# Computing the first token tile of six experts during the attention phase of a fused attention and mixture-of-experts kernel

## The chip, the core and the metric

The kernel runs on one core of a Trainium2 chip. The metric is the device time of one execution in microseconds (us), the median over the timed runs. The core has a matrix engine (TensorE, PE in the profile), a vector engine (VectorE, DVE), a scalar engine (ScalarE, ACT), a general engine (GpSimd, POOL) and a queue engine (SyncE, SP) that here only issues transfers. Each engine executes its own instructions in the order in which they were laid down; instructions of different engines wait for each other through semaphores.

## What is computed

The reference has two blocks. The first is a gated linear attention: for each of 4 batches and 8 heads a complex 48 by 48 state decays by a per-channel factor and takes in an outer product at each of 768 steps.

```python
mag = np.sqrt(a_re * a_re + a_im * a_im)
scale = np.minimum(mag, 0.999) / (mag + 1e-06)
a_re_n, a_im_n = (a_re * scale, a_im * scale)
for t in range(S):
    ar, ai = (a_re_n[:, :, t, :, None], a_im_n[:, :, t, :, None])
    new_re = ar * S_re - ai * S_im
    new_im = ar * S_im + ai * S_re
    kv = np.einsum('bhd,bhe->bhde', k[:, :, t], v[:, :, t])
    S_re, S_im = (new_re + kv, new_im)
    y[:, :, t] = np.einsum('bhd,bhde->bhe', q[:, :, t], S_re)
```

The output, 3072 tokens of 384 numbers, goes into a mixture of 8 experts. Each token goes to the one expert with the largest of 8 logits; the expert is a two-layer network with a hidden width of 1024.

```python
logits = x @ w_gate
expert_idx = np.argmax(logits, axis=1)
# for each expert e, over the tokens that chose it:
h = np.maximum(x_sorted[lo:hi] @ w1[e], 0.0)
y_sorted[lo:hi] = h @ w2[e]
# in the tokens' own order, times the softmax weight of the chosen expert:
return (gate_w[:, None] * y).astype(np.float32)
```

All of it is in 32-bit floats. A matmul on 32-bit operands stands in the trace as two matmul instructions, so that the 24 matmuls of an expert's first layer are 48 lines of the trace.

## The kernel before

**Attention.** The tokens are cut into 24 tiles of 128 (`NT`); tile `g` is chunk `s = g // 4` of batch `b = g % 4`. Two tiles are a unit (`U = 2`), so there are 12 units, and four tiles, one chunk of all batches, are a group (`GR = 4`). The loop `for u in range(NU + 1)` (L498) is a hand-written software pipeline. In iteration `u` it does the decay work of unit `u + 1` (`decay_steps`, `decay_angle`), the cumulative sums of unit `u` by matmul (`decay_sums`, `angle_sums`: tiles `csl` and `cst`), the sines (`rotation`), and then, for the two tiles of unit `u - 1`, `scores(g)` and, one tile later, `outputs(g - 1)`. `scores` multiplies Q and K by their decays on POOL and DVE (`product`, L317), transposes them on PE through the PSUM pool `psT` (two buffers, one bank each), copies them out on ACT or DVE, and makes the attention block `at`, which DVE masks (L424). `outputs` makes `y` from `am` and the state `G`, transposes it, and computes the router's logits (`logits`, L327). All eight PSUM banks are taken by the attention's pools.

**Routing.** After a group of four tiles, `route` (L355) works out for each token its expert (`choose`), its rank within the expert (a running count `cx` and a matmul with a triangle of ones) and from that the row in a DRAM buffer `xs` with `CAP = 448` rows for each expert. Tokens are written there by `put` (L390), an indirect transfer on POOL, one for each tile; one is issued in each call of `scores` (L408). The last group's `route` is called with `end=True` after the loop (L539): it first sets the counts to at least `FIRST = 256`, so that no token of the last group falls into an expert's first 256 rows. That is what makes the first two tiles of an expert complete ahead of the last group. A row that no token took was blanked beforehand (`blank`) and its result is dropped by the bounds check of the scatter. A token with rank 448 or more would set `ov`, and then a slow path (`others`, L770) would run behind the kernel.

**Experts.** After the attention its pools are closed (L542), and the experts are done one after another (L663). `gather` (L475) reads the expert's rows from `xs`; `turn` (L555) transposes them; `expert` (L579) makes the first layer, `hps`, in 8 slices of the hidden width with 3 accumulating matmuls each, all token columns at once (448 columns; relu on DVE and ACT in turn), and the second layer, `yps`, tile by tile: three full tiles of 128 tokens with 8 matmuls of 384 columns each, and a half tile of 64 tokens whose 8 matmuls run in pairs beside each other. `scatter` (L569) writes each tile of results to its tokens' rows. Expert 0 is done in two parts: tiles 0 and 1 first (256 columns, gathered at L538 before the last group is routed), then the remaining tile and a half (192 columns, `rest0`, L661). Beside experts 1 to 6 run checks of the decay inputs on ACT and POOL (`range_check`, L630).

**Weights.** An expert's weights are 1536 KB for each layer. `load_w` (L153) puts them into one of two buffers, by `e % 2`. Expert 0's are loaded in seven pieces during units 4 to 10 of the attention (L533), expert 1's at the end of the attention, and those of expert `e + 2` when expert `e` is done.

**Order.** The order on each engine is made when the kernel is built: a scheduler takes the instructions by their place in the program and by when they are expected to be ready, so an instruction that is ready may be laid down ahead of one that stands before it in the program. `queue` (L147) forces one instruction behind another. Once built, the order is fixed.

Of the kernel before, what the change touches and what calls it, by code (L numbers as in the profile page):

```python
# [20 lines left out]
P = 128  # L21
# [16 lines left out]
def kernel(  # L38
# [26 lines left out]
    CAP = CT * P - HT  # L65
    FIRST = 2 * P
    NS = E * CAP
    GR = B
# [14 lines left out]
    wp = [ctx.enter_context(tc.tile_pool(name="wp", bufs=1)), None]  # L83
    gp = ctx.enter_context(tc.tile_pool(name="gp", bufs=2))

# [38 lines left out]
    nc.vector.memset(cx[:, 0], 0.0)  # L124
    base = const([P, E], "base")
    rev = const([P, E], "rev")
    nc.gpsimd.iota(rev, pattern=[[-1, E]], base=E, channel_multiplier=0, allow_small_or_imprecise_dtypes=True)
# [24 lines left out]

    def load_w(e, parts=None):  # L153

        if e not in W_T:
            W_T[e] = [
                wp[e % 2].tile([P, n, w], FP, tag=nm, name=nm + "t") for nm, n, w in (("w1", KD, F), ("w2", KF, DM))
            ]
        a, b = W_T[e]
        w1e, w2e = w1[e].rearrange("(i p) f -> p i f", p=P), w2[e].rearrange("(i p) d -> p i d", p=P)  # L160
        if parts is None:
            nc.sync.dma_start(out=a, in_=w1e)
            T["w"] = nc.sync.dma_start(out=b, in_=w2e)
        else:
            for i in parts:
                o, x, i = (a, w1e, slice(i, i + 1)) if i < KD else (b, w2e, slice(2 * (i - KD), 2 * (i - KD) + 2))
                queue(nc.sync.dma_start(out=o[:, i], in_=x[:, i]), T["ld"])
# [6 lines left out]
    un = att.enter_context(tc.tile_pool(name="un", bufs=2))  # L174
    ch = att.enter_context(tc.tile_pool(name="ch", bufs=2))
    psM = att.enter_context(tc.tile_pool(name="psM", bufs=1, space=PSUM))
    psT = att.enter_context(tc.tile_pool(name="psT", bufs=2, space=PSUM))
# [177 lines left out]
    def route(j, end):  # L355
# [3 lines left out]
        tt, ts, stt = nc.vector.tensor_tensor, nc.vector.tensor_scalar, nc.vector.scalar_tensor_tensor  # L359
        choose(j, n)  # L360
        oh = xl.tile([P, n, E], BF, tag="oh", name="oh")
        tt(out=oh, in0=bc(rev, 1, n), in1=bc(fst[:, sl], 2, E), op=OP.is_equal)
# [39 lines left out]
    def scores(g):  # L402
# [4 lines left out]
        K = product(u, c, "K", "k", "Ei")  # L407
        if T["put"]:  # L408
            queue(T["put"].pop(0)(), T["K"])
        qts, ats = [], []  # L410
# [23 lines left out]
    def outputs(g):  # L434
# [38 lines left out]
        logits(xt, g)  # L473

    def gather(s, sizes):  # L475

        n = len(sizes)
        xg = gp.tile([P, n, XW], FP, tag="xg", padded_shape=[P, CT, XW], name="xg")
        f = sum(m == P for m in sizes)
        nc.sync.dma_start(out=xg[:, :f], in_=xs[s : s + f * P].rearrange("(i p) c -> p i c", p=P))  # L480
        if f < n:
            nc.sync.dma_start(out=xg[0 : sizes[f], f], in_=xs[s + f * P : s + f * P + sizes[f]])
        return xg
# [14 lines left out]
    for u in range(NU + 1):  # L498
# [19 lines left out]
        else:  # L518
            table("natural_log_exp_and_others")
            for g in T.pop("done", []):  # L520
                T["put"] += route(g, False)
        for g in range((u - 1) * U, u * U):
            if g >= 0:
                scores(g)
            if g > 0:
                outputs(g - 1)
                if g % B == 0:
                    T["done"] = [g - B]
        if u == 1:
            blank()  # L530
        if u + 2 < NU:
            load_a(u + 2)
        if NU - 8 <= u < NU - 1:  # L533
            load_w(0, [u - (NU - 8)])
    outputs(NT - 1)
    for f in T["put"]:
        f()
    own0 = gather(0, [P] * (FIRST // P))  # L538
    for f in route(NT - GR, True):  # L539
        f()  # L540

    att.close()  # L542


    wp[1] = ctx.enter_context(tc.tile_pool(name="wp1", bufs=1))
    load_w(1)
    xp = ctx.enter_context(tc.tile_pool(name="xp", bufs=2))
# [7 lines left out]
    def turn(sizes, xg):  # L555
# [11 lines left out]
        return xt  # L567

    def scatter(y, idx, m):  # L569
        return nc.gpsimd.indirect_dma_start(  # L570
            out=out,
            out_offset=bass.IndirectOffsetOnAxis(ap=idx, axis=0),
            in_=y[0:m],
            in_offset=None,
            bounds_check=N - 1,
            oob_is_err=False,
        )

# [82 lines left out]
    rest0 = [P] * ((CAP - FIRST) // P) + [HT]  # L661
    own = [P] * (CT - 1) + [HT]
    for e in range(E):  # L663
        if e == 0:
            part = [([P] * (FIRST // P), own0), (rest0, gather(FIRST, rest0))]
        else:
            part = [(own, xg)]
        for i, (sizes, g) in enumerate(part):
            xt = turn(sizes, g)
            if i == len(part) - 1 and e + 1 < E:  # L670
                xg = gather((e + 1) * CAP, own)
            todo = []
            if i == len(part) - 1 and 1 <= e < E - 1:
                todo = [lambda b, i=i: range_check(i, b) for i in range(NC) if i % (E - 2) == e - 1]
            expert(sizes, xt, *W_T[e], g, todo)
        if e + 2 < E:
            load_w(e + 2)
        for i in range(NC):
            if i % (E - 2) == e:
                range_load(i)  # L680
        if e == E - 2:
            verdict()
# [152 lines left out]
```

## Time and profile before

| | |
|---|---|
| median of three runs | 647.17 us |
| span of the profiled execution | 648.5 us |
| PE busy | 577.9 us (89%) |
| ACT, DVE, POOL busy | 277.8, 238.3, 215.0 us |
| DMA | 79.74 MB, mean 123 GB/s |
| last logits of the attention copied out (DVE L336) | at 327.0 us |
| first expert's first `hps` matmul | at 327.5 us |
| last matmul | ends at about 638.5 us |

A busy time on PE runs from the start of a matmul to the end of its results, and consecutive matmuls overlap; the distance from one start to the next is shorter than the duration that a row gives. The page also lists the share of the full TensorE clock that was granted (PEclk).

A unit of the attention is followed in the trace by its second sine on ACT (`CS<-f`), which appears once in each unit. For units 6 to 11 these start at 173.8, 195.4, 225.3, 246.9, 279.1 and 298.8 us (times rounded). Right after its second sine a unit's `scores` begin, which stand in iteration `u + 1` of the loop, where the change puts `first` and `second` ahead of them. A stretch from one such time to the next holds one unit's worth of work; the last stretch runs from 298.8 us to the first expert. These six stretches are where the six early tiles would lie.

### The profile page before, as it was taken

How to read it: one execution, taken by the hardware profiler on the slowest of the kernel's cores; microseconds unless marked ns; L12 is line 12 of the kernel's file. 1: busy time of each engine (PE TensorE's matmuls, PEld its weight loads, DVE VectorE, ACT ScalarE, POOL GpSimd, SP SyncE). 2: the span in 40 equal slices, each digit the busy share in tenths (PEclk: the TensorE clock that was granted, in tenths of full speed). 3: DMA queues.
4: the chain of work that ended last, by engine and by line, in shares of the span. 5: the costliest groups of instructions: out<-in, count | busy, mean ns of one | idle time of the engine just before them, and what ended most of it. 6: DMA issues, size and time to landing. Idle time of an engine off the chain costs nothing. (4 is left out here: it accounts for less than half of the span.)

```text
span 648.5 us, 8554 instructions
## 1 busy us (share of the span) xinstructions
PE 577.9 (89%) x3319; PEld 378.7 (58%) x3319; DVE 238.3 (37%) x487; ACT 277.8 (43%) x467; POOL 215.0 (33%) x206
## 2 busy tenths in 40 slices
PE   1496989889699699799999999999999999999993
PEld 0184767668478477588776555555555555555551
DVE  2354657547557547658231211212121021211210
ACT  4656964763666466475210115152341614225100
POOL 3544155351563553632212105032140512405111
PEclk9998899969899899899989999999999999999998
DMA  9999864652743813205203543735425373430000
GB/s 163 210 340 178 124 131 80 151 108 50 159 109 75 161 39 75 62 14 196 73 26 107 201 150 118 252 109 210 137 80 207 109 261 110 152 114 25 10 12 30
DMA packets 151673, 79.74 MB, mean 123 GB/s; under 512 B 130134, under 2 KB 141927, under 8 KB 151624
## 3 DMA queue, kind: packets, MB, share of 16 engines
q1 hardware_dynamic: 143168, 63.75, 41.3%
q0 software_dynamic: 4736, 15.20, 6.9%
q10 hardware_dynamic: 3720, 0.16, 0.4%
q8 instruction: 28, 0.46, 0.3%
q14 instruction: 21, 0.17, 0.1%
HBM read 63.74 MB, written 15.98 MB: 123 GB/s over the span
## 5 line engine op out<-in xcount | busy, mean ns | idle before, releaser
L75 PE MATMUL hps<-xt,w1t 128*128 128x448 f32 (+2 forms) x432 | 148.1, 503 | 0.0
L75 PE MATMUL yps<-w2t,ht 128*128 128x384 f32 (+1 forms) x512 | 147.2, 488 | 0.3 <-DVE y L603 0.3
L75 PEld LDWEIGHTS yps<-w2t,ht 128*128 128x128 f32 (+1 forms) x512 | 81.4, 177 | 64.5 <-issue 15.0
L75 PEld LDWEIGHTS hps<-xt,w1t 128*128 128x128 f32 x432 | 80.8, 192 | 61.8 <-issue 58.7
L588 ACT ACTIVATE ht<-hps 128x448 f32<-128x448 f32 (+2 forms) x36 | 18.1, 502 | 136.1 <-PE hps L75 136.1
L75 PE MATMUL at<-qt,kt 96*128 96x128 f32 x384 | 57.1, 295 | 18.1 <-ACT qt L78 9.4
L75 PEld LDWEIGHTS at<-qt,kt 96*128 96x128 f32 x384 | 50.3, 203 | 28.8 <-ACT qt L78 12.9
L570 POOL DMA_INDIRECT out_dram<-y,xg x32 | 30.9, 967 | 93.0 <-DVE y L603 44.6
L641 POOL TENSOR_TENSOR cs<-cs,cw 128x768 f32<-128x768 f32 x12 | 21.6, 1804 | 117.4 <-ACT cw L637 117.4
L592 DVE TENSOR_SCALAR ht<-hps 128x448 f32<-128x448 f32 (+2 forms) x36 | 20.6, 573 | 103.4 <-PE hps L75 103.4
L603 DVE TENSOR_SCALAR y<-yps,xg 128x384 f32<-128x384 f32 x24 | 14.8, 617 | 118.4 <-PE yps L75 118.4
L320 POOL TENSOR_TENSOR Qe<-q,E 128x384 f32<-128x384 f32 x24 | 23.9, 997 | 82.3 <-ACT E L185 68.6
L75 PE MATMUL y<-am,v 128*64 128x128 f32 x384 | 49.1, 288 | 0.0
L424 DVE TENSOR_TENSOR am<-at,tri 128x512 f32<-128x512 f32 x48 | 33.0, 688 | 33.3 <-PE at L75 33.1
L75 PE MATMUL csl<-A,tri_half 128*128 128x384 f32 x48 | 24.8, 602 | 21.1 <-DVE A L238 18.5
L391 POOL DMA_INDIRECT xs<-x,to x24 | 24.4, 1016 | 57.2 <-DMA xs<-x,to 39.3
L75 PE MATMUL y<-qt,G 96*64 96x128 f32 x320 | 42.1, 280 | 0.0
L416 PE MATMUL tp<-ident,Q 128*96 128x128 f32 x192 | 34.2, 298 | 3.7 <-DVE Q L324 3.7
L75 PE MATMUL dk<-v,K 128*96 128x48 f32 x320 | 33.9, 259 | 2.4 <-DVE t L454 2.4
L75 PEld LDWEIGHTS y<-am,v 128*64 128x64 f32 x384 | 30.0, 138 | 9.7 <-issue 7.4
L78 ACT COPY qt<-tp 96x512 f32<-96x512 f32 x48 | 27.0, 581 | 20.1 <-PE tp L416 18.8
L191 ACT ACT_TABLE_LOAD x27 | 34.6, 1283 | 2.2 <-PEq L821 0.8
(123 smaller groups left out, 805.9 us busy)
## 6 DMA issues: line engine op xcount, KB each, us to landing
w1t<-in_moe_w_dram SPq DMA_DIRECT2D x7, 1536.0 KB
w2t<-in_moe_w_dram SPq DMA_DIRECT2D x7, 1536.0 KB
xs<-zrow POOLq DMA_DIRECT2D x1, 5404.0 KB, 22.4
ar<-in_a_re_dram SPq DMA_DIRECT2D x12, 384.0 KB
ai<-in_a_im_dram SPq DMA_DIRECT2D x12, 384.0 KB
q<-in_q_dram SPq DMA_DIRECT2D x12, 384.0 KB
k<-in_k_dram SPq DMA_DIRECT2D x12, 384.0 KB
v<-in_v_dram SPq DMA_DIRECT2D x12, 384.0 KB
```

What stands on the lines that cost most here:

```text
L75: return nc.tensor.matmul(o, lhsT=lhsT, rhs=rhs, start=start, stop=stop, skip_group_check=True)
L78: (nc.scalar.copy if i % 2 else nc.vector.tensor_copy)(out=o, in_=in_)
L191: ins = nc.scalar.preload_act_table_set(name)
L320: T[nm] = nc.gpsimd.tensor_tensor(out=e.rearrange("p h d -> p (h d)"), in0=T[src, u][:, sl], in1=T[dec, u][:, sl], op=OP.mult)
L391: return nc.gpsimd.indirect_dma_start(out=xs[:, :], out_offset=bass.IndirectOffsetOnAxis(ap=to[:, i : i + 1], axis=0), in_=x[:, i], in_off ...
L416: nc.tensor.transpose(out=tp[0:DD, j], in_=X[:, hg * 4 + j], identity=ident)
L424: nc.vector.tensor_tensor(out=am, in0=at, in1=bc(tri, 1, 4), op=OP.mult)
L570: return nc.gpsimd.indirect_dma_start(out=out, out_offset=bass.IndirectOffsetOnAxis(ap=idx, axis=0), in_=y[0:m], in_offset=None, bounds_ch ...
L588: relu = nc.scalar.activation(out=ht[:, f], in_=ps, func=AF.Relu)
L592: nc.vector.tensor_scalar(out=ht[:, f], in0=ps, scalar1=0.0, scalar2=None, op0=OP.max)
L603: nc.vector.tensor_scalar(out=y, in0=ps, scalar1=gate, scalar2=None, op0=OP.mult)
L641: nc.gpsimd.tensor_tensor(out=s, in0=s, in1=w, op=OP.add)
```

## The change

It computes the first tile of 128 tokens of the experts 0 to 5 (`EARLY`) within the attention phase, one expert in each of the loop's iterations 7 to 12, and takes these tiles out of the expert phase. For this the first tile has to be complete early. After two groups (1024 of the 3072 tokens) are routed, the third `route` sets the counts of the six experts to at least 128 (the tile is closed), so that later tokens go to later rows. The purpose is to use time that PE spends waiting in the attention phase.

The parts are these. The tile is read from `xs` by `early_gather`, issued in the iteration before. `first` does its three transposes, one copy on ACT, 24 matmuls of 128 columns for the first layer (the result in two tiles of `psT`, each emptied by one relu, on ACT and on DVE), and it stands ahead of the first `scores` of the iteration. `second` does 8 matmuls of 384 columns, one DVE multiplication by the gate and a scatter, and stands ahead of the second `scores`. The weights of experts 0 to 5 go one after another through a single buffer during the attention. Since expert 5's are there when the attention ends, the expert phase begins with expert 5, goes on with 6 and 7, and then does 0 to 4, whose weights are loaded a second time. In the expert phase the six experts have 320 columns in place of 448 and two full tiles in place of three. Expert 5's first part is now a single tile of 128, its second part is as expert 0's was. Puts are issued two for each `scores` in the first four groups, and the pool `gp` of the gathered tiles is opened after the attention's pools are closed.

```diff
+    EARLY = range(6)
...
-    def load_w(e, parts=None):
-
-        if e not in W_T:
+    def load_w(e, parts=None, buf=0, new=True):
+
+        if new:
             W_T[e] = [
-                wp[e % 2].tile([P, n, w], FP, tag=nm, name=nm + "t") for nm, n, w in (("w1", KD, F), ("w2", KF, DM))
+                wp[buf].tile([P, n, w], FP, tag=nm, name=nm + "t") for nm, n, w in (("w1", KD, F), ("w2", KF, DM))
             ]
...
+        if j == 2 * GR:
+
+            pc = psL.tile([P, E], FP, tag="mm", padded_shape=[P, 512], name="pc")
+            mm(pc, ones_b, cx[:, j])
+            ts(out=base, in0=pc, scalar1=float(P), scalar2=-float(P), op0=OP.min, op1=OP.add)
+            ne = len(EARLY)
+            stt(out=cx[:, j, :ne], in0=base[:, :ne], scalar=lead, in1=cx[:, j, :ne], op0=OP.mult, op1=OP.add)
...
-        if T["put"]:
-            queue(T["put"].pop(0)(), T["K"])
+        for _ in range(2 if g < 4 * B else 1):
+            if T["put"]:
+                queue(T["put"].pop(0)(), T["K"])
...
+    def early_gather(e):
+        xg = fl.tile([P, XW], FP, tag="xg", name="fxg", bufs=2)
+        queue(nc.sync.dma_start(out=xg, in_=xs[e * CAP : e * CAP + P]), T["ld"])
+        T["fx", e] = xg
+
+    def early(e):
...
+        def first():
+            tp = psT.tile([P, 4, P], FP, tag="tp", name="ftp")
+            for d in range(KD):
+                nc.tensor.transpose(out=tp[:, d], in_=xg[:, d * P : (d + 1) * P], identity=ident)
+            xt = fl.tile([P, KD, P], FP, tag="xt", name="fxt")
+            nc.scalar.copy(out=xt, in_=tp[:, 0:KD])
+            for z in range(2):
+                ps = psT.tile([P, 4, P], FP, tag="tp", name="fhp")
+                for i in range(4):
+                    f = 4 * z + i
+                    for d in range(KD):
+                        mm(ps[:, i], wa[:, d, f * P : (f + 1) * P], xt[:, d], d == 0, d == KD - 1)
+                if z:
+                    nc.vector.tensor_scalar(out=ht[:, 4:8], in0=ps, scalar1=0.0, scalar2=None, op0=OP.max)
+                else:
+                    nc.scalar.activation(out=ht[:, 0:4], in_=ps, func=AF.Relu)
+
+        def second():
+            ps = psT.tile([P, 4, P], FP, tag="tp", name="fyp").rearrange("p a b -> p (a b)")[:, :DM]
+            y = fl.tile([P, DM], FP, tag="y", name="fy", bufs=2)
+            for f in range(KF):
+                mm(ps, ht[:, f], wb[:, f], f == 0, f == KF - 1)
+            nc.vector.tensor_scalar(out=y, in0=ps, scalar1=xg[:, DM : DM + 1], scalar2=None, op0=OP.mult)
+            scatter(y, xg[:, DM + 1 : DM + 2].bitcast(I32), P)
...
+        e = u - 7
+        if e >= 0:
+            steps = early(e)
         for g in range((u - 1) * U, u * U):
+            if e >= 0:
+                steps[g % U]()
...
-        if NU - 8 <= u < NU - 1:
-            load_w(0, [u - (NU - 8)])
+        if 3 <= u < 7:
+            load_w(0, [2 * u - 6, 2 * u - 5] if u < 6 else [6], new=u == 3)
+        if 6 <= u < NU:
+            early_gather(u - 6)
+        if 7 <= u < NU:
+            load_w(u - 6)
     outputs(NT - 1)
     for f in T["put"]:
         f()
-    own0 = gather(0, [P] * (FIRST // P))
+    att.close()
+    gp = ctx.enter_context(tc.tile_pool(name="gp", bufs=2))
+    order = [EARLY[-1], *range(len(EARLY), E), *EARLY[:-1]]
+    own0 = gather(order[0] * CAP + P, [P] * (FIRST // P - 1))
     for f in route(NT - GR, True):
         f()
...
-    for e in range(E):
-        if e == 0:
-            part = [([P] * (FIRST // P), own0), (rest0, gather(FIRST, rest0))]
-        else:
-            part = [(own, xg)]
+    xg = own0
+    for n, e in enumerate(order):
+        own = [P] * (CT - 2 if e in EARLY else CT - 1) + [HT]
+        part = [(own, xg)]
+        if n == 0:
+            part = [([P] * (FIRST // P - 1), xg), (rest0, gather(e * CAP + FIRST, rest0))]
...
-        if e + 2 < E:
-            load_w(e + 2)
+        if n + 2 < E:
+            load_w(order[n + 2], buf=n % 2)
```

## The prediction

> **What bounds the kernel now.** I read first the busy times in stretches (one row for each attention unit from the sixth on, then the handover to the experts, then the experts). Columns: stretch, its length, busy us and count of PE, weight loads, DVE, ACT, POOL, granted clock, DMA share, GB/s.
>
> ```profile
> 173.80:195.40 21.60, 19.41 (x183) 14.88 (x179) 12.53 (x21) 15.18 (x27) 11.70 (x11) 1.00 0.45 99
> 195.40:225.30 29.90, 24.97 (x226) 19.85 (x226) 19.30 (x44) 15.52 (x28) 12.65 (x12) 0.94 0.60 116
> 225.30:246.90 21.60, 19.44 (x183) 14.92 (x180) 12.51 (x21) 15.15 (x27) 11.98 (x11) 1.00 0.21 44
> 246.90:279.10 32.20, 28.60 (x250) 23.14 (x250) 20.57 (x47) 17.23 (x32) 13.96 (x13) 0.89 0.34 75
> 279.10:298.80 19.70, 19.70 (x182) 15.60 (x184) 11.97 (x24) 12.43 (x24) 7.35 (x9) 1.00 0.09 20
> 298.80:327.50 28.70, 26.11 (x275) 21.04 (x272) 12.53 (x38) 11.99 (x25) 4.14 (x5) 0.98 0.38 140
> 327.50:349.50 22.00, 22.00 (x85) 15.96 (x84) 5.67 (x28) 1.76 (x5) 5.08 (x6) 0.95 0.17 59
> 349.50:367.20 17.70, 17.29 (x88) 12.52 (x86) 3.28 (x8) 1.64 (x5) 1.95 (x2) 1.00 0.44 145
> 367.20:648.50 281.30, 270.20 (x872) 143.99 (x870) 45.99 (x83) 82.77 (x139) 71.40 (x53) 0.99 0.36 126
> ```
>
> The experts are bound by PE alone. The attention is bound mostly by PE as well: the six units take 153.7 us, of which PE is busy 138.2, and the next engine, DVE, 89.4. One unit (19.7 us) has no PE idle time at all; the long ones (29.9, 32.2) have 3.6 to 4.9 us.
>
> Next, the timeline of PE in an expert (start, us, matmuls):
>
> ```profile
> 407.94 18.31 PE L75 MATMUL hps<-xt,w1t 128*128 128x448 f32 x48
> 426.08 18.37 PE L75 MATMUL yps<-w2t,ht 128*128 128x384 f32 x64
> 444.38 2.22 PE L561 MATMUL tp<-ident,xg 128*128 128x128 f32 x12
> 446.54 18.31 PE L75 MATMUL hps<-xt,w1t 128*128 128x448 f32 x48
> ```
>
> An expert takes 446.54 - 407.94 = 38.6 us without a gap. Last, the handover, on PE and on POOL:
>
> ```profile
> 339.17 10.48 PE L75 MATMUL yps<-w2t,ht 128*128 128x384 f32 x32
> 349.49 0.94 PE L561 MATMUL tp<-ident,xg 128*128 128x128 f32 x4
> 351.30 8.07 PE L75 MATMUL hps<-xt,w1t 128*128 128x192 f32 x48
> ```
>
> ```profile
> 333.75 0.97 POOL L391 DMA_INDIRECT xs<-x,to  x1 [4.70 <-DVE ht L592]
> 344.06 0.98 POOL L391 DMA_INDIRECT xs<-x,to  x1 [2.38 <-DMA xs<-x,to]
> ```
>
> The last group's four puts go out one behind the landing of the other, from 333.75 to 344.06 us; the gather of the remaining rows can only follow (issued 346.7). PE gets the transposes of that gather at 349.49, just as the 256-column part is used up. So 327.5 to 349.5 is bound by a chain of latencies, with PE work that happens to be as long.
>
> [...] eight `at` matmuls (128 columns) lie 0.89 us apart from the next group, 112 ns each. [...] the same eight matmuls at twice the time after a wait of 3.46 us. [...] the expert phase's relus come without a table load after 300.1 us. I therefore charge none for the early relu.
>
> ```profile
> 220.28 1.97 PE L75 MATMUL at<-qt,kt 96*128 96x128 f32 x8 [3.46 <-ACT qt L78]
> 232.85 1.06 PE L75 MATMUL at<-qt,kt 96*128 96x128 f32 x8
> ```
>
> **What it removes.** In an early expert, 48 first-layer passes shrink from 448 to 320 columns. Passes lie 18.14/48 = 378 ns apart at 448 columns and 7.9/48 = 165 ns at 192, so 0.83 ns a column: 128 columns less save 106 ns, 48 times, 5.1 us. One tile of second layer is 16 passes of 10.32/32 = 323 ns, 5.2 us. Three of 12 transposes are 0.5 us. Sum 10.8 us, and 38.6 becomes 27.8. This holds in full for experts 0 to 4: 54 us. For expert 5 it brings nothing. Its second part has 192 columns, as expert 0's had, and starts when the puts have landed; only the work ahead of it shrinks from 22 to about 11 us, and PE then waits some 11 us for the chain. [...] **2 us lost** (0 to 4).
>
> **What it adds on PE.** In each of six units 48 passes of 128 columns at 112 ns (5.4 us), 16 passes of 384 at 323 ns (5.2 us), 3 transposes (0.4 us), and some 0.2 us at the changes between them: 11.2 us, six times, **67 us**. So PE does more work than before; the change pays only as far as this lies in time that PE lost.
>
> **How much PE time is free.** Idle: 153.7 - 138.2 = 15.5 us. Half clock: 0.06 x 29.9 + 0.11 x 32.2 = 5.3 us, which fuller PE work would win back. Ends of matmuls that count as busy but in which another could have started: about 270 - 112 = 160 ns ahead of each wait, and an estimate of six waits a unit gives 6 us. Together 27 us. The early work is ready long ahead, comes in passes of 0.1 to 0.3 us and can be laid into waits, so I take nine tenths, **24 us**. Two bounds. The groups of PE in this stretch, at their shortest start-to-start distances, are 216 `at` at 0.112 us, 444 `y` at 0.055, 204 transposes at 0.11, 144 `dk` at 0.087, 40 of 384 columns at 0.40, and 62 `tpx`, 112 `lt` and some 57 small ones for 16.5: 116 us, which leaves at most 38 us. But by the same distances the dense unit would be 17.6 us and took 19.7, so a tenth is lost at the changes between groups however full PE is; that puts the free time at 153.7 - 1.12 x 116 = 24 us, near my value. The lower bound is none at all. The attention then grows by 67 - 24 = **43 us** (29 to 67).
>
> **What waits behind it.** ACT gets a copy and a relu (0.5 and 0.6 us by the 512-column copies), DVE a relu and a product (0.7 and 0.6), POOL a scatter of 1.0 us; each has 9 us or more idle in a unit, so nothing. The `psT` bank is held by a half layer for 24 x 0.112 = 2.7 us, leaving one for the Q and K transposes; while it is held, PE itself is busy, so I charge nothing. A scatter waits for `y` on POOL, and behind it the products Qe and Ke wait; POOL is idle for up to 10.4 us ahead of a Qe, so that too is hidden. Weights: 3.1 MB more in each of five units. By the experts' 0.36 of the DMA engines at 126 GB/s, full use is 350 GB/s: 9 us of a unit's 25, on top of shares of 0.09 to 0.60. That fits. The loads wait on SP for the matmuls that free the single buffer, and the attention's loads queue behind them. Each has about a unit of lead, so nothing; the range has to cover a miss. The double puts and the closing of the tile (one small matmul and two DVE instructions of 0.2 us) are under 1 us. No overflow is to be feared: from the reference's inputs the fullest expert has 421 tokens, the closing adds at most 23 rows (expert 0, to 377), and 448 fit.
>
> **In the expert phase** the check on ACT runs 14.3 us from the last relu (426.7 to 441.0), beside 18.3 us of second layer. With 13.1 us it pokes out and delays the next expert's transposed copy by about 1 us, in the two to four early experts that have such checks: **3 us** (0 to 5). An expert has 27.8 us for its 5.2 MB of weights, rows and checks, 187 GB/s of 350: no bound.
>
> **Sum:** 647.2 - 54 + 43 + 2 + 3 = 641.2; I say **641 us**.
>
> **Rivals.**
> *A, the waits are filled deeper.* The start-to-start bound is nearer the truth: 36 us are used, the growth is 31: 647.2 - 54 + 31 + 5 = **629 us**. For it: the units alternate between 20 and 30 us with much the same work, which looks like a recurrence between groups of tiles and not like PE. Against it: the dense unit shows no idle time at 19.7 us, and work already packed there has no more room.
> *B, slower: the new waits stop the attention.* PE is in order; if the weights or the gathered tile come late behind other SP transfers, or `psT` holds up the transposes, the early work finds no gap and adds waits. With 2 us of such waits a unit and none of the 24 us used: 647.2 - 54 + 67 + 12 + 5 = **677 us**; with half of the slack used, 665. For it: one weight buffer, one PSUM pool for all. Against it: a whole unit of lead for the loads, and a share of DMA under 0.6.
> *C, a draw:* PE fills only 10 us: 647.2 - 54 + 57 + 5 = **655 us**. For it: the order is fixed when the kernel is built, and real waits fall elsewhere than the expected ones.
>
> **Chances.** Forecast (634 to 648): 0.42. A (below 634): 0.28. C (648 to 660): 0.18. B: 0.12. Faster by over 2% means below 634.2: A and a hundredth of the forecast, 0.29; slower means above 660.1, B, 0.12; within 2% the remaining 0.59. The range leaves out the deep end of A and the most of B: 624 to 658.
>
> **What would show it.** The attention's last logits copy at 327 + 43 = 370 us; PE busy without gaps in the six stretches, their clock at 1.00; PE idle for about 11 us in the handover; 27.8 us from one early expert to the next; 48 `hps` passes of 320 columns with a mean start distance near 270 ns. The forecast is wrong if the last logits come before 360 or after 385, or if waits on the early weights (PE or weight loads behind `w1t`, `w2t`) come up by more than 2 us a unit.

## The result, and the profile after

The kernel after the change takes 665.95 us (median of four runs, 665.6 to 668.04) against 647.75 for the kernel before on the same chip (647.11 to 654.73): a ratio of 1.027, with a 95% interval of 1.020 to 1.033. It is **slower by 2.7%**. The forecast was 641 us, with a range of 624 to 658. Some executions of a kernel fall into a slower state with a lower granted clock (the kernel before took 656.9 us at 0.952 in one run, where its median of 647.68 came at 0.973); the ratios and intervals here and below leave these out and so differ a little from the quotients of the medians.

The busy times in stretches of the changed kernel come first, cut as the prediction cut them: six units of the attention, each from its second sine to the next one's, then the handover, the first expert's second part, and the other experts. Columns: stretch, its length, busy us and count of PE, weight loads, DVE, ACT, POOL, granted clock, DMA share, GB/s.

```profile
172.60:195.60 23.00, 20.82 (x179) 16.71 (x179) 12.28 (x20) 14.72 (x27) 10.82 (x12) 0.93 0.38 89
195.60:234.20 38.60, 35.13 (x284) 28.68 (x283) 20.92 (x47) 16.60 (x29) 12.94 (x12) 0.96 0.60 156
234.20:266.10 31.90, 31.20 (x260) 24.86 (x259) 15.72 (x24) 16.66 (x29) 13.22 (x13) 1.00 0.55 158
266.10:305.40 39.30, 35.52 (x308) 29.80 (x307) 19.82 (x46) 17.32 (x31) 12.95 (x13) 1.00 0.50 144
305.40:336.70 31.30, 31.30 (x250) 24.93 (x249) 12.57 (x21) 13.48 (x25) 10.77 (x12) 0.95 0.32 110
336.70:388.50 51.80, 50.03 (x419) 38.36 (x418) 18.26 (x46) 15.89 (x33) 6.07 (x7) 1.00 0.43 149
388.50:410.50 22.00, 10.91 (x68) 8.26 (x66) 4.92 (x29) 1.23 (x5) 5.06 (x6) 0.86 0.19 60
410.50:431.10 20.60, 20.25 (x86) 15.31 (x86) 2.76 (x7) 1.64 (x5) 0.97 (x1) 0.82 0.32 113
431.10:663.90 232.80, 219.65 (x777) 127.70 (x775) 39.14 (x78) 80.12 (x139) 66.56 (x48) 0.98 0.41 144
```

The six units take 216 us where they took 153. PE is still the only engine near its limit there, and yet it stands idle in five of the six: 2.2, 3.5, 0.7, 3.8 and 1.8 us (length less busy). The share of the DMA engines never passes 0.60. In the handover PE works for 10.9 us of 22.

Three marks split the difference of the spans, 663.9 - 648.5 = 15.4 us (the medians are 18.2 us apart: the traced execution of the kernel before took 650.5 us, some 3 us more than its median, so what is read against this trace may be off by as much):

| stretch | before, us | after, us | difference |
|---|---|---|---|
| start to the last logits copy on DVE | 0 to 327.0 | 0 to 388.9 | +61.9 |
| from there to the first transposes of the remaining rows | to 349.5 | to 410.5 | -0.9 |
| from there to the end | to 648.5 | to 663.9 | -45.6 |

So the expert phase gave back nearly what was forecast (-49), and the attention took half as much again as was forecast (+43). The timeline of PE in the experts of the changed kernel shows the first (start, us, matmuls, the idle time before and what ended it):

```profile
510.11 13.19 PE L76 MATMUL hps<-xt,w1t 128*128 128x320 f32 x48
523.14 13.21 PE L76 MATMUL yps<-w2t,ht 128*128 128x384 f32 x48
536.28 1.86 PE L631 MATMUL tp<-ident,xg 128*128 128x128 f32 x9
538.08 13.54 PE L76 MATMUL hps<-xt,w1t 128*128 128x320 f32 x48
...
594.70 13.53 PE L76 MATMUL hps<-xt,w1t 128*128 128x320 f32 x48
608.07 13.21 PE L76 MATMUL yps<-w2t,ht 128*128 128x384 f32 x48
623.64 0.19 PE L76 MATMUL bp<-two,ones 128*1 128x2 f32 x2 [2.36 <-DVE two L715]
623.77 1.21 PE L631 MATMUL tp<-ident,xg 128*128 128x128 f32 x6
625.49 0.64 PE L631 MATMUL tp<-ident,xg 128*128 128x128 f32 x3 [0.52 <-ACT xt L79]
626.06 14.88 PE L76 MATMUL hps<-xt,w1t 128*128 128x320 f32 x48
```

A shortened expert takes 538.08 - 510.11 = 28.0 us, the next two 28.3 each. The fourth takes 626.06 - 594.70 = 31.4, because the last range check, on ACT, now ends after the expert's PE work, and the matmul `bp` of the verdict (the sum over all checks), which waits for it, stands ahead of the next expert's transposes.

The PE timeline of the handover:

```profile
394.18 5.33 PE L76 MATMUL yps<-w2t,ht 128*128 128x384 f32 x16
410.49 1.13 PE L631 MATMUL tp<-ident,xg 128*128 128x128 f32 x4 [10.98 <-DMA xg<-xs]
411.97 0.78 PE L631 MATMUL tp<-ident,xg 128*128 128x128 f32 x2 [0.34 <-DVE xt L79]
412.67 10.63 PE L76 MATMUL hps<-xt,w1t 128*128 128x192 f32 x48
423.14 8.05 PE L76 MATMUL yps<-w2t,ht 128*128 128x384 f32 x32
431.12 2.22 PE L631 MATMUL tp<-ident,xg 128*128 128x128 f32 x12
```

PE is out of work for 11 us until the gather lands, as forecast, and 48 passes of 192 columns take 10.5 us in place of 8.

**Where the attention lost it.** I summed the distances from each PE start to the next (less gaps in which PE stood idle) over the six units. Start-to-start times add up, which busy times of overlapping matmuls do not: the 48 `hps` passes at 510.11 count 13.19 us as busy, and the next group starts 13.03 us after them.

| six units, us | before | after | difference |
|---|---|---|---|
| early work (`ftp`, `fhp`, `fyp`) | 0 | 70.4 | +70.4 |
| idle | 15.5 | 11.9 | -3.6 |
| all other PE work | 137.7 | 133.9 | -3.8 |
| length | 153.2 | 216.2 | +63.0 |

The added work is the 67 us of the forecast, a little more. Of the 24 us of free time that it was to use, it used 7.4. The longest wait of PE that is left in these units shows one thing that keeps free time from being used. First PE, then ACT, in the changed kernel's timeline:

```profile
294.77 1.72 PE L76 MATMUL fhp<-fxt,w1t 128*128 128x128 f32 x14
296.33 0.81 PE L76 MATMUL cst<-ai,tri_turn 128*128 128x384 f32 x2
296.98 3.96 PE L76 MATMUL fhp<-fxt,w1t 128*128 128x128 f32 x34
304.72 0.64 PE L429 MATMUL tp<-ident,Q 128*96 128x128 f32 x4 [3.78 <-ACT fht L523]
```

```profile
298.78 0.84 ACT L190 ACTIVATE R<-R 128x768 f32<-128x768 f32 x1 [4.06 <-POOL R L234]
301.82 0.94 ACT L190 ACTIVATE R<-A,ln2e 128x768 f32<-128x768 f32 x1 [2.19 <-DVE A L238]
302.77 1.28 ACT L196 ACT_TABLE_LOAD   x1
304.07 0.60 ACT L523 ACTIVATE fht<-fhp 128x512 f32<-128x512 f32 x1
```

Both half layers lie in a row (14 + 34 passes) and fill both buffers of `psT`. The first half is complete after its 24th pass, at about 298.3 us. The relu that empties it stands on ACT behind a logarithm and an exponential, which wait for POOL and for DVE, and behind the table load for the sines; it starts at 304.07. Until it ends the next Q transposes have no buffer, and PE idles 3.8 us. Besides this one, two waits of 0.7 us are for a `psT` buffer that is not yet emptied, so that 5.2 of the 11.9 us of idle time are of this kind. In the other five units the relu starts within 1.9 us of the 24th pass, and the first half is emptied before PE comes to the next Q transposes.

ACT, which copies the transposes out, waits too. Engine, line, what it waited for: us in total, times, longest. Before, then after, then e2 of the next section, in which PE idles only 3.1 us:

```profile
ACT qt L78 <- PE tp L416: 8.7, 6, 3.1
```

```profile
ACT qt L79 <- PE tp L429: 39.0, 19, 6.0
```

```profile
ACT qt L78 <- PE tp L416: 37.6, 17, 5.2
```

ACT gets the transposed Q late 19 times in place of 6. But it waits nearly as long in e2, where the added passes found most of the free time. So this wait comes with a fuller PE, and it does not tell a lost gap from a used one.

### The profile page after: what moved, and what is told of

The parts are those of the page before. It is cut to its first block, busy times and chain, and to the rows that moved or that the text cites. A ratio compares the mean times of both kernels' runs of the same rounds, so it can differ in the third digit from the quotient of the medians.

```text
span 663.9 us, 9198 instructions
## 1 busy us (share of the span) xinstructions
PE 582.9 (88%) x3608; PEld 410.4 (62%) x3608; DVE 240.3 (36%) x496; ACT 281.1 (42%) x479; POOL 214.7 (32%) x206
## 4 chain that ended last, share of the span: by engine, by line
PE 68%; ACT 8%; DVE 8%; POOL 7%; issue 4%; DMA 4%; POOLq 0%; SPq 0%; ACTq 0%; DVEq 0%
PE hps L76 18%; PE yps L76 9%; PE at L76 7%; PE tp L429 6%; PE y L76 6%; PE fyp L76 5%; PE fhp L76 4%; PE dk L76 4%; POOL cai L704 2%; PE csl L76 2%; POOL cs L701 2%; PE cst L76 2%; DMA xs<-x,to 2%; PE tpx L480 1%; PE tp L631 1%
## 5 line engine op out<-in xcount | busy, mean ns | idle before, releaser
L76 PE MATMUL hps<-xt,w1t 128*128 128x320 f32 (+3 forms) x432 | 121.9, 442 | 0.2
L76 PE MATMUL yps<-w2t,ht 128*128 128x384 f32 (+1 forms) x416 | 116.2, 488 | 0.0
L76 PEld LDWEIGHTS hps<-xt,w1t 128*128 128x128 f32 x432 | 79.8, 198 | 38.6 <-issue 18.4
L76 PEld LDWEIGHTS yps<-w2t,ht 128*128 128x128 f32 (+1 forms) x416 | 63.1, 174 | 50.2 <-issue 13.7
L648 ACT ACTIVATE ht<-hps 128x320 f32<-128x320 f32 (+3 forms) x36 | 15.5, 431 | 109.7 <-PE hps L76 108.2
L489 POOL DMA_INDIRECT out_dram<-y,xg x26 | 25.1, 965 | 90.8 <-DVE y L663 45.4
L701 POOL TENSOR_TENSOR cs<-cs,cw 128x768 f32<-128x768 f32 x12 | 21.6, 1804 | 81.1 <-ACT cw L697 81.1
L652 DVE TENSOR_SCALAR ht<-hps 128x320 f32<-128x320 f32 (+3 forms) x36 | 17.4, 483 | 81.7 <-PE hps L76 81.7
L663 DVE TENSOR_SCALAR y<-yps,xg 128x384 f32<-128x384 f32 x18 | 11.1, 618 | 92.5 <-PE yps L76 92.5
L429 PE MATMUL tp<-ident,Q 128*96 128x128 f32 x192 | 32.8, 290 | 8.8 <-ACT fht L523 3.8
L76 PE MATMUL fhp<-fxt,w1t 128*128 128x128 f32 x288 | 37.5, 291 | 1.6 <-ACT fxt L513 1.6
L76 PEld LDWEIGHTS fhp<-fxt,w1t 128*128 128x128 f32 x288 | 36.4, 205 | 3.9 <-ACT fxt L513 2.6
```

What stands on the lines that cost most here:

```text
L76: return nc.tensor.matmul(o, lhsT=lhsT, rhs=rhs, start=start, stop=stop, skip_group_check=True)
L429: nc.tensor.transpose(out=tp[0:DD, j], in_=X[:, hg * 4 + j], identity=ident)
L489: return nc.gpsimd.indirect_dma_start(out=out, out_offset=bass.IndirectOffsetOnAxis(ap=idx, axis=0), in_=y[0:m], in_offset=None, bounds_ch ...
L648: relu = nc.scalar.activation(out=ht[:, f], in_=ps, func=AF.Relu)
L652: nc.vector.tensor_scalar(out=ht[:, f], in0=ps, scalar1=0.0, scalar2=None, op0=OP.max)
L701: nc.gpsimd.tensor_tensor(out=s, in0=s, in1=w, op=OP.add)
```

## The experiments

In all of them the length of the attention is taken from the seventh unit's second sine to the last logits copy, because the units before that, in which no early tile is computed, end up to 8.7 us apart from one run to another (170.5 to 179.2). "Used" is the early PE time (start to start) less the growth of this length over the 153.2 us of before: the free time that the early work found. Each length is that of one traced execution.

| run | what | time, us | early PE time | length | growth | used | PE idle |
|---|---|---|---|---|---|---|---|
| after | six tiles, `psT` | 665.95 | 70.4 | 216.2 | 63.0 | 7.4 | 11.9 |
| e1 | a third or less of the passes, `psT` | 628.34 | 18.9 | 177.9 | 24.7 | -5.8 | 18.3 |
| e2 | before, and passes on constants, `psT` | 695.52 | 65.8 | 201.1 | 47.9 | 17.9 | 3.1 |
| e3 | six tiles, `psB` | 648.88 | 66.8 | 199.4 | 46.2 | 20.6 | 2.6 |
| g0 | the same kernel as e3 | 651.64 | 67.5 | 202.7 | 49.4 | 18.1 | 2.7 |
| g4 | only `ftp` in `psB` | 666.07 | 69.4 | 218.1 | 64.9 | 4.5 | 14.6 |
| g9 | only `fhp` in `psB` | 655.51 | 67.8 | 206.6 | 53.4 | 14.4 | 7.0 |
| g3 | few passes, `psB` | 623.23 | 18.1 | 166.4 | 13.2 | 4.9 | 16.4 |
| e4 | five tiles, `psT` | 660.76 | 57.6 | 205.9 | 52.7 | 4.9 | 16.0 |
| g2 | five tiles, `psB`, verdict later | 639.78 | 55.7 | 191.3 | 38.1 | 17.6 | 5.0 |
| g6 | four tiles, as g2 | 643.97 | 45.1 | 187.2 | 34.0 | 11.1 | 8.4 |
| g7 | three tiles, as g2 | 639.12 | 33.5 | 172.5 | 19.3 | 14.2 | 6.7 |
| g5 | two tiles, as g2 | 650.56 | 22.2 | 171.5 | 18.3 | 3.9 | 13.6 |

Times of e1, e2, e3, e4, g3, g4 and g9 are single runs; the others are medians. How far one execution can be trusted shows in two places. The kernel before took from 645.9 to 656.9 us in the repeated runs beside these (654.4 in its one execution beside e1 to e4). And e3 and g0 are one kernel: their lengths differ by 3.3 us with the same idle time, and the granted clock of the whole traced execution is 0.965 in e3 and 0.944 in g0. So a difference of some 3 us between two lengths says nothing.

**Is it the amount of PE work, or the waits that come with it?** Two runs take them apart. e1 keeps every buffer, wait, load and scatter of the change but does 16 of the 48 first-layer passes and 2 of the 16 second-layer passes; the rest of the early products is left out.

```diff
-                    for d in range(KD):
-                        mm(ps[:, i], wa[:, d, f * P : (f + 1) * P], xt[:, d], d == 0, d == KD - 1)
+                    mm(ps[:, i], wa[:, 0, f * P : (f + 1) * P], xt[:, 0])
...
-            for f in range(KF):
-                mm(ps, ht[:, f], wb[:, f], f == 0, f == KF - 1)
+            mm(ps, ht[:, 7], wb[:, 7])
```

> The changed kernel with all its new loads, gathers, copies, relus and scatters, but only 16 of the 48 first-layer passes and 2 of the 16 second-layer passes of each early tile (the rest of the products is left out, so the six early tiles are wrong). In the changed kernel the early passes take 35.9 + 31.8 us of start-to-start time; 51.8 us of it goes. Theory 1 (the attention is bound by PE throughput, what is left of idle time cannot be filled): the last logits copy moves from about 389 to 341 us (337 to 347), the time from 666 to about 618 us. Theory 2 (the new waits on weights, the gathered tile, the PSUM pool and the scatter stretch the attention): the last logits stay above 360 us, the time above 637 us.

Measured: last logits at 351.5 us, a length of 177.9. Only 18.9 us of PE work was added, and the attention grew by 24.7: none of the free time was used, and 5.8 us more were lost. Among the waits of PE in e1 are some for the gathered tile:

```profile
PE ftp L511 <- DMA fxg<-xs: 6.7, 2, 5.9
```

which the full change does not show. Neither theory's number was met (341 us, or over 360, for the last logits). PE's throughput alone would not explain the growth; something that comes with the early tiles keeps PE from the free time.

e2 goes the other way. It is the kernel before with the same passes at the same places and in the same `psT`, on constants: no gather, weights, relu or scatter. Each result is given free by a tiny copy on DVE.

```diff
+    def extra(second):
+        for z in range(1 if second else 2):
+            ps = psT.tile([P, 4, P], FP, tag="tp", name="xps")
+            if second:
+                for f in range(KF):
+                    mm(ps.rearrange("p a b -> p (a b)")[:, :DM], (tri, tri_half)[f % 2], wide, f == 0, f == KF - 1)
+            else:
+                for i in range(4):
+                    for d in range(KD):
+                        mm(ps[:, i], (tri, tri_half)[(3 * i + d) % 2], tri_turn, d == 0, d == KD - 1)
+            nc.vector.tensor_copy(out=junk[:, z : z + 1], in_=ps[:, 0, 0:1])
...
+            if u >= 7:
+                extra(g % U)
```

> The kernel before with the same PE passes added at the same places (48 of 128 columns and 16 of 384 in each of the last six iterations, on constant tiles, through the same PSUM pool), and nothing else of the change: no loads, gathers, copies, scatters, no other routing. One tiny DVE copy empties each PSUM tile. Theory 1: the attention grows by nearly all of the added PE time, 11.3 us each: last logits at 327 + 57 = 384 us (377 to 391), time 704 us (697 to 711). Theory 2: PE passes without the new waits fit into the free time, growth at most 43 us, time below 690 us.

Measured: 65.8 us of passes made the attention 47.9 longer; 17.9 us were used and PE idles 3.1. The time of 695.52 us lies between the two theories (704, or below 690). So most of the free time that the forecast counted is there, and passes without the change's data and waits find it. They use `psT` just as the change does, but each result is begun to be emptied within 1.3 us of its last pass. Sharing the pool is thus not by itself enough to lose the free time.

**Is it `psT`?** e3 moves the three kinds of early result (`ftp`, `fhp`, `fyp`) to the pool of the output's transposes `tpx`, which has one buffer; g0 is the same kernel, timed repeatedly.

```diff
-            tp = psT.tile([P, 4, P], FP, tag="tp", name="ftp")
+            tp = psB.tile([P, 4, P], FP, tag="tp", name="ftp")
...
-                ps = psT.tile([P, 4, P], FP, tag="tp", name="fhp")
+                ps = psB.tile([P, 4, P], FP, tag="tp", name="fhp")
...
-            ps = psT.tile([P, 4, P], FP, tag="tp", name="fyp").rearrange("p a b -> p (a b)")[:, :DM]
+            ps = psB.tile([P, 4, P], FP, tag="tp", name="fyp").rearrange("p a b -> p (a b)")[:, :DM]
```

> The changed kernel, with the early tiles' three PSUM tiles taken from the bank of the token transposes (psB) in place of the pool of the Q and K transposes (psT), so that these keep both buffers. Theory 1: the same within 4 us (662 to 670 us). Theory 2 (the held PSUM buffer stops the Q and K transposes; one wait of 3.8 us behind an early relu is seen): at least 10 us faster, below 656 us.

> The changed kernel with the early tiles in the bank of the token transposes, now timed: 649 us (647 to 652), the same as the kernel before within 1%. If the single look had been chance: back near 666 us.

Measured: 648.88 us in one execution; in repeated runs 651.64 (20 runs, 647.85 to 660.1) against 647.68, a ratio of 1.004 (1.001 to 1.007). Against the changed kernel that is 14.3 us less by the medians. The stretches of e3, cut at the same marks:

```profile
172.80:194.80 22.00, 20.46 (x189) 16.32 (x188) 11.97 (x19) 15.07 (x27) 11.80 (x10) 1.00 0.39 91
194.80:226.40 31.60, 31.60 (x263) 26.20 (x263) 20.43 (x48) 16.43 (x30) 12.52 (x10) 1.00 0.71 181
226.40:256.00 29.60, 29.60 (x245) 23.28 (x245) 13.67 (x21) 16.32 (x28) 11.42 (x11) 1.00 0.62 181
256.00:289.00 33.00, 32.98 (x283) 27.48 (x282) 19.83 (x47) 17.18 (x32) 15.40 (x14) 1.00 0.44 127
289.00:322.80 33.80, 33.80 (x303) 27.76 (x302) 13.51 (x23) 13.82 (x26) 11.20 (x12) 1.00 0.50 147
322.80:372.20 49.40, 48.39 (x420) 38.47 (x420) 17.39 (x46) 14.83 (x31) 8.27 (x9) 1.00 0.44 156
```

This is the picture that the prediction had drawn: four of the six stretches without a gap, the clock at 1.00, last logits at 372.2 (forecast 370), a growth of 46.2 (forecast 43). Against the changed kernel the length falls by 16.8 us (13.5 with g0's trace): 9.3 are idle time, 3.6 the early passes themselves (the `fhp` lie 115 ns apart and not 125), 3.9 other PE work. Much of the last two is the half clock: the changed kernel's shares of 0.93, 0.96 and 0.95 over 23.0, 38.6 and 31.3 us make 4.7 us (an estimate), and e3 has 1.00 throughout. ACT's wait for transposed Q falls from 39.0 us in 19 times:

```profile
ACT qt L79 <- PE tp L429: 24.2, 7, 6.8
```

Moving the pool also moves the order that the build gives the PE instructions, and a pool of one buffer keeps the two half layers apart: in e3's timeline the passes come as 14 + 10, then Q and K transposes, then 24. The run shows what the choice of pool is worth with all that follows from it. It does not tell the buffer's hold apart from the new order. What the changed kernel's trace ties to a full `psT` is 5.2 us of idle time and, behind the wait of 3.8 us, the 0.05 of the clock that is missing over 31.3 us (1.6 us; the clock is 0.50 from 306 to 308 us and 1.00 from 309 on): 6.8 of the 16.8 us, as an estimate. For the other 10 no wait behind `psT` is seen; a kernel that changes the pool and keeps the order was not run.

**Which of the three results?** g4 moves `ftp` alone, g9 `fhp` alone: the first or the second of e3's three edits.

> The changed kernel with only the early tile's transposes in the other bank; the half layers and the second layer stay in the shared pool. In the changed kernel the transposes hold their buffer for 8.8, 11.3, 3.8, 3.7, 2.2 and 1.1 us until ACT copies them out. If this hold is the main part of what the pool costs: last logits at 381 us or sooner, time 658 or less. If the half layers and the second layer are: last logits at 385 us or later, time 662 or more.

> The changed kernel with only the two half layers in the other bank, transposes and second layer in the shared pool. In the changed kernel the two halves are laid down in a row and take both buffers, and the next Q transposes wait for the relu (3.8 us at one place). If this is what the pool costs: the attention from the seventh unit's second sine to the last logits is at most 205 us (199 with all three in the other bank, 216 with none), time 656 us or less. If the second layer's hold is the main part: 210 us or more, time 660 or more.

Measured: g4 666.07 us with a length of 218.1, as expected if the transposes are not the main part; g9 655.51 with 206.6, where at most 656 and 205 had been expected if the half layers are. The transposes' hold costs nothing that can be seen by itself. In the changed kernel's trace I had seen them keep a buffer up to 11.3 us (from 218.18 till the copy at 229.5), and had suspected them. The half layers bring 9.6 of the 16.8 us. The remaining 7.2 come only when `ftp` and `fyp` move as well; `fyp` alone was not tried. The wait of 3.8 us behind the relu is 3.6 us in g4 and gone in g9.

**Is `psT` all of it?** g3 is e1's few passes in `psB`.

> Few passes (16 and 2 of 48 and 16, the rest of the early products left out) and the other bank together. With few passes in the shared pool the attention grew by 24 us although only 19 us of PE time were added. Theory P (the shared PSUM pool, held while an early tile waits for its copy or relu, is what eats the free PE time): with the bank of its own the 19 us fit into the free time, last logits at 327 to 334 us, time about 608 us. Theory W (other new waits do it: weights, gathered tile, scatter on POOL): last logits at 345 us or later, time over 620 us.

Measured: 623.23 us, last logits at 344.9, so at the mark of theory W and far from theory P. The attention is 166.4 us long, 11.5 less than in e1, so the pool has its part; but it still grows by 13.2 us for 18.1 us of work, where the free time of 18 to 21 us seen in e2 and e3 would hold all of it. So the shared pool is not all of it. PE's own waits and POOL's timeline of g3 show other waits:

```profile
PE fhp L76 <- ACT fht L522: 3.3, 2, 2.1
PE ftp L511 <- DMA fxg<-xs: 3.3, 1, 3.3
```

```profile
282.34 1.02 POOL L403 DMA_INDIRECT xs<-x,to  x1 [1.01 <-DMA xs<-x,to]
293.69 0.97 POOL L403 DMA_INDIRECT xs<-x,to  x1 [10.33 <-DMA fxg<-xs]
294.97 0.97 POOL L489 DMA_INDIRECT out_dram<-fy,fxg  x1 [0.30 <-issue]
295.96 1.02 POOL L325 TENSOR_TENSOR Qe<-q,E 128x384 f32<-128x384 f32 x1
```

A put waits 10.3 us until an early gather has read `xs`, and the unit's Qe, which the Q transposes need, stands behind it on POOL. e3 has the same wait once (10.1 us) and used 20.6 us all the same. That such a wait sets the length in g3 was not tried; it stays open.

**The sixth tile.** e4 leaves expert 5's early tile out, so that the expert phase begins with two tiles as before.

```diff
-    EARLY = range(6)
+    EARLY = range(5)
...
-    order = [EARLY[-1], *range(len(EARLY), E), *EARLY[:-1]]
-    own0 = gather(order[0] * CAP + P, [P] * (FIRST // P - 1))
+    order = [*range(len(EARLY), E), *EARLY]
+    own0 = gather(order[0] * CAP, [P] * (FIRST // P))
...
-            part = [([P] * (FIRST // P - 1), xg), (rest0, gather(e * CAP + FIRST, rest0))]
+            part = [([P] * (FIRST // P), xg), (rest0, gather(e * CAP + FIRST, rest0))]
```

> The changed kernel without the sixth early tile: experts 0 to 4 early, and expert 5 begins the expert phase whole, with a first part of two tiles as in the kernel before; its weights come as in the changed kernel. My reading of the handover (11 us of PE idle there, so that the sixth tile buys nothing and costs its 11 us in the attention): last logits at about 378 us, no idle time over 1 us in the handover, and 653 us (650 to 657) in all. If the sixth tile was worth its place: 664 us or more.

Measured: 660.76 us, some 8 above what was expected; but the first units of this run ended 6.5 us later than in the changed kernel (179.2 against 172.6). The length fell by 10.3 us, and PE has no long wait left in the handover (a wait of 2.2 us stands just before the last logits). So the sixth tile cost 10 us in the attention and brought nothing.

**What the parts make together.** g2 is e4 and e3 in one, with the verdict moved behind the last expert's first layer, so that its matmul no longer stands ahead of that expert's transposes.

```diff
+            if n == E - 1:
+                todo = [lambda b: verdict()]
...
-        if n == E - 2:
-            verdict()
```

> Other bank, five early tiles (expert 5 whole at the start of the expert phase), and the verdict on the checks laid behind the last expert's first layer in place of ahead of it. Sixth tile: 11 us of attention saved, the handover's idle time filled; verdict: 2.4 us of PE idle and 1.6 us at half clock saved. 649 - 11 - 4 = 634 us (630 to 639), 2% faster than before. If the sixth tile lies in free time once the bank is its own: 644 us or more.

Measured: 639.78 us (635.2 to 643.86), at the upper end of what was expected (630 to 639); ratio to before 0.989 (0.982 to 0.995). The PE timeline of its handover has no wait for the gather:

```profile
374.91 10.48 PE L76 MATMUL yps<-w2t,ht 128*128 128x384 f32 x32
385.23 0.94 PE L631 MATMUL tp<-ident,xg 128*128 128x128 f32 x4
```

and in the experts the last check still holds up the last expert, by another way (DVE's transposed copy stands behind the check's ending):

```profile
596.36 0.64 PE L631 MATMUL tp<-ident,xg 128*128 128x128 f32 x3 [2.08 <-DVE xt L79]
```

e4 and g2 have the same five tiles; their lengths, 205.9 and 191.3, show the pool's worth a second time: 14.6 us (g2's trace is of an execution of 635.2 us, its fastest).

**How many tiles?** g5, g6 and g7 are g2 with two tiles (iterations 8 and 10), four (7 to 10) and three (7 to 9). The edit of g7 against g2, where the gathers and weight loads, not shown, follow the same table:

```diff
-    EARLY = range(5)
+    EARLY = range(3)
+    SLOT = {7: 0, 8: 1, 9: 2}
...
-        e = u - 7
-        if e in EARLY:
+        e = SLOT.get(u, -1)
+        if e >= 0:
...
```

> Other bank, verdict behind the last first layer, and only two early tiles, in the iterations 8 and 10, whose work falls into the long units (29.9 and 32.2 us before, with 8.5 us of PE idle and 5.3 us lost to the half clock). Saved in the expert phase 2 x 10.8 = 21.6 us; added in the attention 2 x 11.2 us less what goes into the waits. If the waits of these two units are filled as well as with five tiles (20 of 24 us used over six units, here up to 12): 647.5 - 21.6 + 22.4 - 12 = 636 us. If free time in these units cannot be used by so few tiles (as with the few passes, where 5 us were used): 643 us or more.

> The same with four early tiles in the iterations 7 to 10. Saved 43.2 us, added 44.8 us less what is free in these units (15 to 18 us): 632 us (629 to 637). If the fifth tile is worth having, this is slower than the five-tile version (636 to 640), by up to 4 us; if not, it is equal or faster.

> The same with three early tiles in the iterations 7 to 9. Saved 32.4 us, added 33.6 less 12 to 15 us free: 634 us (631 to 640).

Measured, as ratios to before: two tiles 1.003 (0.999 to 1.008), four 0.989 (0.986 to 0.993), three **0.983** (0.975 to 0.990, 639.12 us, 638.89 to 639.31). Two tiles came out in the worse of the two cases given for them (643 us or more), four 7 us above their range, three within theirs. The free time used is 3.9, 14.2, 11.1, 17.6 and 20.6 us for two, three, four, five and six tiles. The dip at four is one trace's: its execution took 648.58 us where the median is 643.97, and the granted clock over its length is 0.97, where it is 0.98 with three tiles and 1.00 with five. That two tiles found so little is outside such differences, but they also lie in other iterations than the first two of three, so their number is not told apart from their place. Three, four and five tiles are faster than both kernels, by 1 to 2% against before, and which of the three is best the intervals do not decide.

## Why the prediction was wrong

**The removal was right.** 10.8 us a tile: a shortened expert takes 28.0 to 28.3 us, forecast 27.8. The experts 6 and 7, which keep all their tiles, take 38.6 and 38.2.

**The handover was right.** The sixth tile buys nothing: the wait of 11 us is there (10.98), e4 takes it away and gains 10.3 in the attention. The half clock was 2 us in the sum, the author's estimate, and cost 2.9: the second part, from its first transposes to the next expert's first layer, took 22.8 us against 19.85, with a granted clock of 0.82 in its stretch against 1.00.

**The checks were undersized, and one way was missed.** Forecast 3 us (0 to 5). The four shortened experts before the last cost 0.2, 0.5, 0.5 and 3.6 us over 27.8, and the last one's first layer 1.7 at half clock after the wait: 6.5 us. The check does poke out on ACT, as forecast; but its largest cost goes by the verdict's matmul on PE, which the prediction did not name.

**The added PE work was right.** Forecast 67 us; 66.8 in e3, 70.4 in the changed kernel, 2.8 of the excess in `fhp` passes that lie 125 and not 115 ns apart. The 115 ns lie near the 112 ns that the `at` matmuls of before had shown and that the forecast counted. What limits these passes no run shows.

**The free time was there; the step that failed is the one that let the early work get at it.** Of the 24 us of the forecast e3 used 20.6 (g0 18.1) and e2 17.9, and the clock was 1.00 over the length in both, where it was 0.96 before. The changed kernel used 7.4. The failing sentence is "The `psT` bank is held by a half layer for 24 x 0.112 = 2.7 us, leaving one for the Q and K transposes; while it is held, PE itself is busy, so I charge nothing." It counts the hold only while PE fills the buffer. A buffer is held until it is emptied, and that waits for its turn on ACT: from 294.8 to 304.7 us in the place shown, where ACT had other instructions first. Nor does it leave one buffer: the second half takes that as well. Where the sum has nothing for the pool, the choice of the pool was worth 16.8 us by e3's length, 13.5 by g0's and 14.3 by the medians; half layers 9.6 (g9), transposes alone none (g4). That the pool costs this much is shown. It is not shown that the hold is all of this cost: about 6.8 us are tied to full buffers in the trace, and the rest may come from the order of PE's instructions, which changed with the pool.

With 16.8 us the sum is 647.2 - 54 + 43 + 2 + 3 + 16.8 = 658, and with the checks and the half clock at their measured size (4.4 us more) 662, 4 below what was measured. Of the difference 3.2 is e3's growth of 46.2 in place of 43. That it closes says little about the cause, since 16.8 and 3.2 together are by construction the measured growth of 63.0 less 43.

One reading in the same part of the prediction does not hold either. It gives each engine "9 us or more idle in a unit", but by its own rows ACT has 21.6 - 15.18 = 6.4 us in the first unit. And an engine's idle time in a unit does not say when its next instruction has its turn.

**The rivals.** B named this: "`psT` holds up the transposes", at 665 us with half of the slack used, and was given 0.12. That its 665 is the measured 666 is in part luck: it adds 12 us of waits and lets 12 us be used, a growth of 67, and 63.0 was measured. Its other causes did not carry it: no wait on the early weights shows in PE's waits of the six units, and the DMA share never passes 0.60. The prediction listed "one PSUM pool for all" for it, and answered with the lead of the loads, which bears on the weights only. That argument left the pool unanswered. A, in which 36 us would be used, fails: at most 20.6 were used in any of these runs. C, in which only 10 us are filled because the order is fixed when the kernel is built, comes nearest to the 7.4 us used; its 655 us becomes 666 with a growth of 63.0 in place of 57 and the 4.4 us of checks and half clock. Its mechanism is not excluded, since e3 changed the order along with the pool.

By its own tests it fails where it said it would: last logits after 385 us (388.9), clock under 1.00 in three of six units, PE idle in five. The waits on the early weights, its other sign of being wrong, did not come up.

## What to carry to other kernels

Work that is to fill an engine's waits should get its own output buffers, or those of a patient neighbour; here that was worth 14 to 17 us. When a shared buffer is priced, count until the emptying instruction has had its turn on its engine, not until the buffer is full. The free time read from idle time and clock was an upper figure here: of 24 us the runs used between none and 20.6. So try other pools and other numbers of pieces (three did as well as five; two, in other places, found little). And don't shorten work that covers a chain of transfers: the sixth tile took 11 us of work out of such a stretch, and PE waited 11 us there instead.

## What the runs showed of the hardware that was not expected

The half clock cost more than forecast. Granted clock and busy times in two stretches of the changed kernel's handover (columns as in the first view):

```profile
404.10:417.70 13.60, 6.87 (x22) 5.97 (x23) 1.07 (x3) 0.65 (x2) 0.97 (x1) 0.51 0.34 103
417.70:425.00 7.30, 7.30 (x40) 6.58 (x39) 1.07 (x3) 0.99 (x3) 0.00 (x0) 0.99 0.10 12
```

PE resumed at 410.49. From then on it was busy but for one wait of 0.34 us, just before 411.97 (6.87 us of the first row), and the clock stayed at half until about 417.9: 7.4 us. Before the last expert, after waits of 2.36 and 0.52 us, the clock is 0.57 from 626 to 630 and 1.00 from 630 on; twice 0.43 of these 4 us is 3.4 us at half clock. In the trace of before the clock is 0.57 from 220 to 224 us, again 3.4 us, behind the wait of 3.46 us that the prediction shows; and behind a wait of 3.37 us, for ACT's copy of K, it is 0.50 from 272 to 278 us, so 6 us at least. The waits do not rank these lengths, and what makes the difference these runs do not tell.
